# Low parts of one weight matrix on GpSimd, the decoder's first result left in PSUM, a joint first step and a reordered expert stage, in a delta-rule and mixture-of-experts kernel

## The chip, the cores and the metric

One core of a Trainium2 chip runs the whole program. The metric is device time in microseconds (us) of one launch, as a median over runs. Engines: PE is TensorE, PEld its weight load, DVE is VectorE, ACT is ScalarE, POOL is GpSimd, SP is SyncE, which here only issues DMAs.

## What is computed

The reference is a chain of three parts. All inputs arrive as 64-bit floats.

```python
# attention: B, H, S, D = 4, 8, 768, 48, one step per token
k_n = k / (np.linalg.norm(k, axis=-1, keepdims=True) + 1e-06)
for t in range(S):
    y[:, :, t] = np.einsum('bhd,bhde->bhe', q[:, :, t], state)
    v_old = np.einsum('bhde,bhd->bhe', state, kt)
    state = state + bt * np.einsum('bhd,bhe->bhde', kt, vt - v_old)
# first block: x is 3072 x 384, w1 and w2 384 x 1024, w3 1024 x 1024, w_out 1024 x 384
h = (x @ w1) * (x @ w2) @ w3
x = h @ w_out
# second block: 8 experts, the best one for each token
logits = x @ w_gate + modality_bias[modality_id]
e_idx = np.argmax(logits, axis=1)
h = np.maximum(x[mask] @ w1[e], 0.0)
out[mask] = gate_w[mask, None] * (h @ w2[e])
```

## The kernel before, in words

**Engine order.** Every instruction is recorded by a wrapper at line 86, which ties it to the last one of its engine; so each engine keeps the order in which the code was written, and the profile shows L86 for nearly all. A value is kept as two parts, a high one and a low one, and a product takes three matmul passes. ACT casts the high part; the low part is the difference, on DVE (`w34l`, `w`, `sxl`, `hl`, `w2l`, `cl`) or POOL (most of `w1l`).

**Startup** (`startup`, line 553). A list `todo` of 36 tiles of 64-bit words is decoded: tiles 0 to 7 are w_out, the even ones from 8 to 30 and some between are w3, the odd ones from 17 and the last are w1 and w2. `scalar` (line 615) makes on ACT the magnitude `mag` from the high words and the low bits in `out` (shown as `TT`). `vector` (line 631) joins them on DVE with two scalar_tensor_tensor instructions, "the pair" below: the first reads `mag` and `out` and writes `out`, the second reads the raw high words and `out` and writes `out`. `mag` lies in PSUM, for tiles 10 to 32 in a ring "AB" of two buffers. `use` (line 638) folds w3 with w_out into `pw` on PE, or splits a tile of w1 or w2 into its parts; the splits wait in a list `after` that `flush` empties some ticks later. `tick(n)` (line 685) issues: `scalar(n + 1)`, `vector(n)`, the parts that are due, new loads, `use(n)`. The last tile of w3 is tile 30, at the index called `folded`.

**Attention.** 768 tokens go in 12 steps s of 64, for 16 pairs of heads; two steps are a unit, whose triangular matrix `TT` is found on DVE (`tmp`, `Tt`). X[s % 2] holds the state in its first 48 columns and the queries in the other 64 (`queries`, line 409, two DMAs a step). `chain_k` (line 445) multiplies with the keys: for s > 1 state and queries jointly into four PSUM tiles `pkq` (64x112 a matmul), two from the ring `ps` of two buffers, then two from `pc`, also of two. `R` takes the state part, `mask_parts` (line 479) multiplies the query part by a mask on DVE, half of it in slot 0 of the step, half in slot 1. For step 1 state and queries are apart: `pk` in `chain_k`, then `pq` in `masked` (line 417). `chain_u` (`pu`), `chain_y` (`py`) and `chain_s` (`pS`) take both buffers of `pc` each time. POOL's `clear` zeroes 32 rows of X[1] behind the last fold, which had w_out there.

**First block** (`moe1`). Its 12 steps of 8 slots f run beside the attention steps; `slot` (line 167) puts `chain_k` into slot 0, `chain_u` into slot 2 or 3, `chain_y` into 4. The matmuls are `pAB` (9 a matrix) and `px`. Tiles 34 and 35 are decoded in its step 0.

**Second block** (`moe2`, line 1081). 14 slots i of up to 256 tokens of one expert, 8 parts f each (`back`, line 1248): 9 `ph` matmuls, then 6 `spy`. Beside slot i, `ahead` (line 1120) prepares slot i + 1: `weights` splits w1 and w2 of the expert, `tokens2` transposes gathered tokens `xg` (`spt` on PE, `sxh` on ACT, `sxl` on DVE). In slot 0 `late` (line 1086) also places the last tokens: `hot` on DVE, `pl` on PE, `list` on DVE.

Of the kernel before, what the change touches and what calls it, by code (L numbers as in the profile page):

```python
# [8 lines left out]
F32 = mybir.dt.float32  # L9
# [3 lines left out]
I32 = mybir.dt.int32  # L13
# [8 lines left out]
P = 128  # L22
# [83 lines left out]
class Kernel:  # L106
# [60 lines left out]
    def slot(self, s, f):  # L167

        if s >= NS:
            return  # L170
        u, c = divmod(s, US)
        self.at(s + f / FC)
        more = u + 1 < NUNIT
        if f == 0:
            self.chain_k(s)
            if s == 1:
                self.queries(1)
                self.queries(2)
        elif f == 1:
            if c == 0:  # L180
                list(self.merge1(u))
                next(self.work, None)
                if more:
                    self.work = self.inverse(u + 1)
            if s > 1:
                list(self.masks)
        elif f == 2:
            list(self.chain_u(s) if c else self.merge2(u))
            if s == 1:
                list(self.masked(s))  # L190
            if s + 1 < NS:
                self.values(s + 1)
        elif f == 3:
            if c == 0:
                list(self.chain_u(s))
            if c == 1 and u + 2 < NUNIT:
                self.keys(u + 2)
        elif f == 4:
            list(self.chain_y(s))
        elif f == 5:  # L200
            if s + 2 < NS:
                self.queries(s + 2)
            if c == 1 and u + 2 < NUNIT:
                self.prep(u + 2, range(0, NP, HP))
        elif f == 6:
            if s + 1 < NS:
                list(self.chain_s(s))
        elif f == 7:
            if s + 2 < NS:
                self.tokens(s + 2)  # L210
            if c == 1 and u + 2 < NUNIT:
                self.prep(u + 2, range(NP, NU, HP))
# [204 lines left out]
    def masked(self, s):  # L417

        nc, ps = self.nc, self.ps
        kT, W, n0 = self.st[s // US]["kT"], self.st["W", s], s % US * NP  # L420
        mb = self.mask.unsqueeze(1).to_broadcast([P, HP, C])
        todo = []
        for a in range(0, NP, HP):
            pq = ps.tile([P, HP, C], F32, tag="ps", name="pq")
            for n in range(HP):
                for h in range(2):
                    o, w = (1 - h) * C, h * C
                    nc.tensor.matmul(pq[o:o + C, n], kT[w:w + C, n0 + a + n], W[w:w + C, h, a + n], start=True, stop=True)
            todo.append((a, pq))
        yield  # L430
        for a, pq in todo:
            for h in range(2):
                o = (1 - h) * C
                if s < 1:
                    nc.scalar.copy(W[o:o + C, h, a:a + HP], pq[o:o + C])
                    nc.gpsimd.affine_select(out=W[o:o + C, h, a:a + HP], in_=W[o:o + C, h, a:a + HP], pattern=[[0, HP], [1, C]], compare_op=ALU.is_gt, fill=0.0, base=0, channel_multiplier=-1)
                    continue
                nc.vector.tensor_tensor(out=W[o:o + C, h, a:a + HP], in0=pq[o:o + C], in1=mb[o:o + C], op=ALU.mult)

    halves = range(0, NP, HP)  # L440

# [3 lines left out]
    def chain_k(self, s):  # L445

        nc, a1, pc = self.nc, self.a1, self.pc
        kT, n0, vt = self.st[s // US]["kT"], s % US * NP, self.st["v", s]
        self.scaled(s)
        if s == 0:  # L450
            self.R = vt
            return
        X = self.X[self.xi]
        R = a1.tile([P, NP, D], F32, tag="R", name="R")
        if s > 1:
            todo = []
            for q, a in enumerate(range(0, NP, NQ)):
                pool, tag = ((self.ps, "ps"), (pc, "pc"))[q // 2]
                pk = pool.tile([P, NQ, D + C], F32, tag=tag, name="pkq")
                for m in range(NQ):  # L460
                    for h in range(2):
                        o, w = (1 - h) * C, h * C
                        nc.tensor.matmul(pk[o:o + C, m], kT[w:w + C, n0 + a + m], X[w:w + C, h, a + m], start=True, stop=True)
                todo.append((a, pk))
            for a, pk in todo:
                nc.vector.tensor_tensor(out=R[:, a:a + NQ], in0=vt[:, a:a + NQ], in1=pk[:, :, 0:D], op=ALU.subtract)
            self.R = R
            self.masks = self.mask_parts(s, todo)
            next(self.masks)
            return  # L470
        for a in self.halves:
            pk = pc.tile([P, HP, D], F32, tag="pc", name="pk")
            for n, m, h in self.tiles(a):
                o, w = (1 - h) * C, h * C
                nc.tensor.matmul(pk[o:o + C, m], kT[w:w + C, n0 + n], X[w:w + C, h, n, 0:D], start=True, stop=True)
            nc.vector.tensor_tensor(out=R[:, a:a + HP], in0=vt[:, a:a + HP], in1=pk, op=ALU.subtract)
        self.R = R

    def mask_parts(self, s, todo):

        W = self.st["W", s]
        mb = self.mask.unsqueeze(1).to_broadcast([P, NQ, C])
        for q, (a, pk) in enumerate(todo):
            for h in range(2):
                o = (1 - h) * C
                self.nc.vector.tensor_tensor(out=W[o:o + C, h, a:a + NQ], in0=pk[o:o + C, :, D:], in1=mb[o:o + C], op=ALU.mult)
            if q == 1:
                yield
# [72 lines left out]
    def startup(self):  # L561
# [22 lines left out]
        last = {f"w{m}1{kk}": todo.index(("w", (m, 1, kk))) for kk in range(KC) for m in range(2)}  # L584

        free = [f"w{m}1{kk}" for kk in range(KC) for m in range(2)] + ["x0", "x1", "xr"]
        raw, out, mag, after = {}, {}, {}, []
        issued = [0]

        def issue(upto=100):  # L590
# [39 lines left out]

        def vector(n):
            L, Hw, tag = raw.pop(n)
            o, stt = out[n].bitcast(I32), nc.vector.scalar_tensor_tensor
            stt(out=o, in0=mag[n].bitcast(I32), scalar=3, in1=o, op0=ALU.logical_shift_left, op1=ALU.bitwise_or)
            stt(out=o, in0=Hw, scalar=-2147483648, in1=o, op0=ALU.bitwise_and, op1=ALU.bitwise_or)
            if tag != "x0" or n < FC:
                free.append(tag)

        def use(n):
            kind, x = todo[n]  # L640
            due = n + 1 if kind == "w" else min(n + 2, FC) if kind == "o" else n + (2 if n < FC + AHEAD else 4)
            if kind == "o":
                pt = pm.tile([P, KC, P], F32, tag="AB", name="wot", bufs=2)
                for kk in range(KC):
# [12 lines left out]
            elif kind == "3":  # L657
# [6 lines left out]
                if g < half - 1:  # L664
                    return

                def f():
                    nc.scalar.copy(self.w34[0][:, r], pw)
                    nc.vector.tensor_tensor(out=self.w34[1][:, r], in0=pw, in1=self.w34[0][:, r].bitcast(F32), op=ALU.subtract)
            else:  # L670
                m, g, kk = x
                t = wp.tile([P, 2, DCH], F32R, tag=f"w{m}{g}{kk}", name=f"w{m + 1}")
                hi, lo = self.w12[m][0][g][kk], self.w12[m][1][g][kk] = t[:, 0], t[:, 1]

                def f():
                    nc.scalar.copy(hi, out[n])
                    nc.vector.tensor_tensor(out=lo, in0=out[n], in1=hi.bitcast(F32), op=ALU.subtract)
            after.append((due, f))

        def flush(n):  # L680
            now = [f for due, f in after if due <= n]
            after[:] = [x for x in after if x[0] > n]
            for f in now:
                f()

        def tick(n):
            self.n = n
            if n >= NSTART - 2:
                flush(n)
            scalar(n + 1)  # L690
            vector(n)
            flush(n)
            issue()
            use(n)

# [39 lines left out]
            do.setdefault(FC + 8 + x, []).append(lambda: next(rs, None))  # L735
        do.setdefault(t + 4, []).append(lambda: self.parts_x(0))
        folded = todo.index(("3", K3 - 1))
        do.setdefault(folded, []).append(self.clear)
        do.setdefault(folded + 1, []).append(lambda: split(self.chain_s(0)))
        do.setdefault(NSTART - 1, []).extend([lambda: self.tokens(1), lambda: self.tokens(2)])  # L740
        for n in range(-1, NSTART):
# [339 lines left out]
    def moe2(self, early, cur):  # L1081
# [3 lines left out]

        def late():
            yield
            yield from self.place(NT // MT - 1)
            yield
            yield from self.listed()  # L1090
            yield
            yield from self.late_slots()
# [22 lines left out]
        def ahead(i):  # L1115

            self.upto = i + 2
            toks = iter(self.tokens2(todo[i + 1], states[i + 1])) if i + 1 < len(kinds) else iter(())

            def step(tok, n):  # L1120
                for _ in range(n):
                    next(work, None)
                if tok:
                    next(toks, None)

            return step, toks
# [129 lines left out]
    def back(self, i, mi, ahead):  # L1256
# [11 lines left out]
        for f in range(FC):  # L1268
# [9 lines left out]
            hl = s3.tile([P, SLOT], F32R, tag="hl", name="hl", bufs=SLAG + 2)  # L1278
            nc.scalar.activation(hh, ph, AF.Relu)
            nc.vector.scalar_tensor_tensor(out=hl, in0=ph, scalar=0.0, in1=hh.bitcast(F32), op0=ALU.max, op1=ALU.subtract)  # L1280
            ahead(f in (1, 2, 3), 1 + (f < 3 if i == 0 else f > 4))
            if i < NEARLY:
                next(self.late, None)
            elif i > NEARLY + 1:
# [105 lines left out]
```

## Time and profile before

| | us |
|---|---|
| median of 3 runs (lowest to highest) | 841.74 (840.85 to 842.69) |
| the profiled execution | 841.03 |
| its span in the profile | 839.3 |
| around the span | 1.73 |
| PE busy | 786.3 (94%) |
| DVE busy | 618.8 (74%) |
| ACT busy | 408.9 (49%) |
| POOL busy | 165.6 (20%) |

The profiled execution stands 0.71 below the median. The times in the profile count from the start of the span. Startup lasts to about 121, steps 1 to 11 to about 565, and the second block takes the rest. Busy time includes work that overlaps.

### The profile page before, as it was taken

The numbers are of one execution on the slowest core, as the hardware profiler recorded it, in microseconds if no ns is written. First come the engines' busy times: TensorE is split into PE (matmuls) and PEld (weight loads), VectorE is DVE, ScalarE is ACT, GpSimd is POOL, SyncE is SP. The second block draws the span as 40 slices with busy tenths as digits, with TensorE's granted clock in tenths as the row PEclk, the third lists the DMA queues.
The fourth block names the chain that finished last, engine by engine and source line by source line (L and its number), as shares of the span: only waits on it lengthen the run. The fifth ranks groups of instructions, "written<-read, shape, count | busy, mean of one in ns | idle before, by whom it ended". The sixth has DMA issues, their size and how long they took to land.

```text
span 839.3 us, 23624 instructions
## 1 busy us (share of the span) xinstructions
PE 786.3 (94%) x9583; PEld 730.6 (87%) x9583; DVE 618.8 (74%) x1573; ACT 408.9 (49%) x863; POOL 165.6 (20%) x172
## 2 busy tenths in 40 slices
PE   5797789999999999999999999999899999999994
PEld 5664468999999899989998999999799999999983
DVE  5998889769777976897689864567886778677651
ACT  6467673562546154524543353334455655655541
POOL 3021121100000001000100000013254654645420
PEclk8598899999999999999999999999999999999997
DMA  9952563314121421133021401047457678677610
GB/s 310 280 176 87 151 161 102 75 35 120 54 51 38 116 65 40 40 115 82 23 65 39 102 13 31 27 131 222 151 177 246 215 249 258 227 225 238 220 56 6
DMA packets 71812, 105.34 MB, mean 126 GB/s; under 512 B 33988, under 2 KB 53332, under 8 KB 71696
## 3 DMA queue, kind: packets, MB, share of 16 engines
q1 hardware_dynamic: 64464, 88.35, 34.7%
q0 software_dynamic: 4064, 11.06, 3.9%
q10 hardware_dynamic: 3168, 4.34, 1.5%
q8 instruction: 77, 1.26, 0.6%
q14 instruction: 39, 0.32, 0.1%
HBM read 89.15 MB, written 10.63 MB: 119 GB/s over the span
## 4 chain that ended last, share of the span: by engine, by line
PE 46%; DVE 26%; issue 11%; ACT 7%; POOL 4%; DMA 3%; SPq 1%; POOLq 0%; DVEq 0%; ACTq 0%
PE pAB L86 13%; PE px L86 9%; PE ph L86 7%; PE spy L86 4%; DVE tmp L86 4%; DVE Tt L86 4%; DVE X L86 3%; DVE TT L86 2%; PE pw L86 2%; DVE Ab L86 2%; ACT TT L86 2%; PE pkq L86 2%; PE pg L86 2%; DVE a L86 2%; PE py L86 2%
## 5 line engine op out<-in xcount | busy, mean ns | idle before, releaser
L86 PE MATMUL pAB<-x,w 128*128 128x256 f32 x1728 | 228.8, 286 | 0.0
L86 PEld LDWEIGHTS pAB<-x,w 128*128 128x128 f32 x1728 | 213.9, 191 | 4.4
L86 ACT CAST ch<-a 128x256 fp32r<-128x256 f32 x96 | 39.0, 406 | 116.4 <-DVE a L86 116.4
L86 ACT COPY a<-pAB 128x256 f32<-128x256 f32 x96 | 35.6, 371 | 116.9 <-PE pAB L86 104.3
L86 DVE TENSOR_TENSOR a<-a,pAB 128x256 f32<-128x256 f32 x96 | 40.0, 416 | 65.6 <-ACT a L86 65.3
L86 PE MATMUL ph<-sxh,w1h 128*128 128x256 f32 x288 | 82.5, 286 | 0.5 <-DVE hl L86 0.5
L86 ACT ACTIVATE hh<-ph 128x256 fp32r<-128x256 f32 x96 | 37.0, 385 | 91.7 <-PE ph L86 91.5
L86 PE MATMUL ph<-sxl,w1h 128*128 128x256 f32 x288 | 81.2, 282 | 0.0
L86 PE MATMUL ph<-sxh,w1l 128*128 128x256 f32 x288 | 81.2, 282 | 0.0
L86 DVE SCALAR_TENSOR_TENSOR hl<-ph,hh 128x256 fp32r<-128x256 f32 x96 | 40.3, 420 | 41.0 <-ACT hh L86 40.5
L86 DVE TENSOR_TENSOR Tt<-tmp,Tt 128x31 f32<-128x31 f32 (+15 forms) x186 | 64.3, 346 | 6.4
L86 DVE TENSOR_TENSOR w2l<-r,w2h 128x768 fp32r<-128x768 f32 x56 | 59.5, 1074 | 12.2 <-ACT w2h L86 11.9
L86 DVE TENSOR_TENSOR tmp<-Ab,Tt 128x31 f32<-128x31 f32 (+15 forms) x186 | 65.4, 352 | 3.0
L86 PE MATMUL px<-w34h,ch 128*128 128x392 f32 x192 | 65.6, 342 | 0.0
L86 PE MATMUL px<-w34h,cl 128*128 128x392 f32 x192 | 65.3, 340 | 0.0
L86 PE MATMUL px<-w34l,ch 128*128 128x392 f32 x192 | 65.2, 339 | 0.0
L86 POOL TENSOR_TENSOR w1l<-r,w1h 128x512 fp32r<-128x512 f32 x39 | 51.0, 1327 | 49.9 <-ACT w1h L86 49.6
L86 DVE TENSOR_TENSOR cl<-a,ch 128x256 fp32r<-128x256 f32 x96 | 43.0, 447 | 20.1 <-ACT ch L86 19.3
L86 PEld LDWEIGHTS ph<-sxh,w1h 128*128 128x128 f32 x288 | 54.7, 190 | 1.3 <-DVE hl L86 1.1
L86 PEld LDWEIGHTS ph<-sxh,w1l 128*128 128x128 f32 x288 | 54.8, 190 | 0.0
L86 PEld LDWEIGHTS ph<-sxl,w1h 128*128 128x128 f32 x288 | 54.6, 190 | 0.0
L86 ACT CAST w1h<-r 128x512 fp32r<-128x512 f32 x84 | 49.5, 615 | 2.9 <-DMA r<-in_e_w_dram 2.5
(269 smaller groups left out, 1677.7 us busy)
## 6 DMA issues: line engine op xcount, KB each, us to landing
r<-in_e_w_dram SPq DMA_DIRECT2D x42, 512.0 KB, 4.7
r<-in_e_w_dram SPq DMA_DIRECT2D x56, 384.0 KB, 3.9
raw<-in_w_dram SPq DMA_DIRECT2D x28, 512.0 KB, 4.6
kT<-in_kt_dram SPq DMA_DIRECT2D x12, 512.0 KB, 4.5
X<-in_q_dram SPq DMA_DIRECT2D x24, 256.0 KB, 4.8
vt<-in_v_dram SPq DMA_DIRECT2D x12, 384.0 KB, 4.7
kb<-in_kb_dram SPq DMA_DIRECT2D x12, 384.0 KB, 4.7
x2d<-xr ACTq DMA_DIRECT2D x22, 192.5 KB, 2.8
```

The lines of the kernel that those rows point to most:

```text
L86: x = f(*a, **kw)
```

## The change

1. In `vector` the first result of the decoder stays in `mag`, in place, and the second instruction reads it there. Tiles from 33 on keep `mag` in SBUF.
2. In `tick` the high parts that are due stand ahead of that tick's `mag` and `TT` on ACT; the low parts still follow the pair.
3. The low parts of w1's tiles 17, 21, 25 and 29 go to POOL.
4. The queries of steps 1 and 2 are fetched right behind tile 30. Step 1 is joint too (`pkq`), and its mask is a copy on ACT and an affine_select on POOL in place of DVE's product.
5. The four `pkq` tiles come from `ps`, `ps`, `pc`, `pc` in even steps and from `pc`, `pc`, `ps`, `ps` in odd steps.
6. In the second block `pl` and `list` of slot 0 come one f later; in slot 0 the tokens of slot 1 stand ahead of its weights; in slot 2 the transposes are at f = 3, 4, 5 in place of 1, 2, 3.

```diff
 def slot(self, s, f):
         if f == 0:
             self.chain_k(s)
-            if s == 1:
-                self.queries(1)
-                self.queries(2)
...
-            if s > 1:
-                list(self.masks)
+            list(self.masks)
...
-            if s == 1:
-                list(self.masked(s))
...
 def chain_k(self, s):
-            pool, tag = ((self.ps, "ps"), (pc, "pc"))[q // 2]
+            pool, tag = ((self.ps, "ps"), (pc, "pc"))[(q // 2 + s) % 2]
...
 def mask_parts(self, s, todo):
+                if s == 1:
+                    self.nc.scalar.copy(W[o:o + C, h, a:a + NQ], pk[o:o + C, :, D:])
+                    self.nc.gpsimd.affine_select(out=W[o:o + C, h, a:a + NQ], in_=W[o:o + C, h, a:a + NQ], pattern=[[0, NQ], [1, C]], compare_op=ALU.is_gt, fill=0.0, base=0, channel_multiplier=-1)
+                    continue
...
 def vector(n):
-            stt(out=o, in0=mag[n].bitcast(I32), scalar=3, in1=o, op0=ALU.logical_shift_left, op1=ALU.bitwise_or)
-            stt(out=o, in0=Hw, scalar=-2147483648, in1=o, op0=ALU.bitwise_and, op1=ALU.bitwise_or)
+            stt(out=m, in0=m, scalar=3, in1=o, op0=ALU.logical_shift_left, op1=ALU.bitwise_or)
+            stt(out=o, in0=Hw, scalar=-2147483648, in1=m, op0=ALU.bitwise_and, op1=ALU.bitwise_or)
...
+                low.append((n + 1, lambda: (nc.gpsimd if not m and n < NSTART - 3 else nc.vector).tensor_tensor(out=lo, in0=out[n], in1=hi.bitcast(F32), op=ALU.subtract)))
...
 def tick(n):
+            for f in due(n, (high,)):
+                f()
             scalar(n + 1)
             vector(n)
-            flush(n)
+            for f in due(n, (low, after)):
+                f()
             issue()
             use(n)
...
-        do.setdefault(folded, []).append(self.clear)
+        do.setdefault(folded, []).extend([self.clear, lambda: self.queries(1), lambda: self.queries(2)])
...
 def late():
             yield
-            yield from self.place(NT // MT - 1)
+            last = self.place(NT // MT - 1)
+            next(last)
             yield
+            next(last)
+            yield
+            yield
+            list(last)
             yield from self.listed()
...
 def step(tok, n):
+                if tok and i == 0:
+                    next(toks, None)
                 for _ in range(n):
                     next(work, None)
-                if tok:
+                if tok and i > 0:
                     next(toks, None)
...
-            ahead(f in (1, 2, 3), 1 + (f < 3 if i == 0 else f > 4))
+            ahead(f - 2 * (i == 2) in (1, 2, 3), 1 + (f < 3 if i == 0 else f > 4))
```

SP at the end of startup, where it issues the last loads of raw words (`raw`), the keys of later steps (`kb`) and the queries (X_91 is X[1], for step 1, and X_90 is X[0], for step 2):

```order
 L86 DMA vt<-in_v_dram 128x768
-L86 DMA raw<-in_w_dram 128x512 x13
-L86 DMA kb<-in_kb_dram 128x768 x2
+L86 DMA raw<-in_w_dram 128x512 x12
 L86 DMA X_91<-in_q_dram 64x16x64 x2
 L86 DMA X_90<-in_q_dram 64x16x64 x2
+L86 DMA raw<-in_w_dram 128x512
+L86 DMA kb<-in_kb_dram 128x768 x2
```

The four loads of queries have moved ahead of the last raw tile and of two loads of keys, which now stand behind them.

POOL in startup, behind the stores of step 0's output (`x<-yT`); the names w_... are w1's tiles, TT_94 holds decoded tiles:

```order
 L86 DMA x<-yT 32x256
+L86 TENSOR_TENSOR w_1034<-TT_94,w_1034 128x512
+L86 TENSOR_TENSOR w_1087<-TT_94,w_1087 128x512
+L86 TENSOR_TENSOR w_1124<-TT_94,w_1124 128x512
 L86 MEMSET X_91 32x32x48 x2
 L86 TENSOR_TENSOR vt<-vt,rb 128x768
+L86 AFFINE_SELECT X_91<-X_91 64x4x64 x8
```

Three of the four low parts now stand between the stores and the zeroing of X[1], and the eight selects of step 1 behind it.

DVE in slot 0 of the second block, from the comparisons `hot` of the last tokens to the `list` that is made of them:

```order
 L86 TENSOR_SCALAR hot<-cols,hi 128x192
 L86 SCALAR_TENSOR_TENSOR hl<-ph,hh 128x256
-L86 TENSOR_TENSOR w2l<-r,w2h 128x768
-L86 TENSOR_TENSOR sxl<-spt,sxh 128x256
+L86 TENSOR_TENSOR sxl<-spt,sxh 128x256
+L86 TENSOR_TENSOR w2l<-r,w2h 128x768
+L86 SCALAR_TENSOR_TENSOR hl<-ph,hh 128x256
+L86 TENSOR_TENSOR w2l<-r,w2h 128x768
 L86 TENSOR_TENSOR list<-pl,list 128x192
-L86 SCALAR_TENSOR_TENSOR hl<-ph,hh 128x256
-L86 TENSOR_TENSOR w2l<-r,w2h 128x768
 L86 TENSOR_SCALAR shift<-list 128x192
```

Here `sxl` has moved ahead of `w2l`, and `list` behind one more `hl` and `w2l`.

## Rows read from the trace of the kernel before

**Rows 1.** The page: span, busy time of each engine

```profile
span 839.3 us, 23624 instructions
...
PE 786.3 (94%) x9583; PEld 730.6 (87%) x9583; DVE 618.8 (74%) x1573; ACT 408.9 (49%) x863; POOL 165.6 (20%) x172
```

**Rows 2.** Windows: stretch and length; busy PE, PEld, DVE, ACT, POOL; granted clock; DMA

```profile
57.00:121.00 64.00, 49.82 (x666) 31.60 (x666) 55.09 (x108) 44.24 (x81) 12.73 (x25) 0.89 0.45 141
159.00:565.00 406.00, 400.68 (x6214) 381.23 (x6214) 303.22 (x914) 175.18 (x373) 17.89 (x16) 1.00 0.22 60
...
597.00:601.00 4.00, 3.86 (x18) 3.92 (x18) 1.89 (x5) 0.00 (x0) 0.00 (x0) 0.57 0.54 215
```

**Rows 3.** Waits of PE from 120 to 560: us in total, times, longest

```profile
PE pu L86 <- DVE X L86: 4.1, 4, 1.4
PE py L86 <- DVE X L86: 1.6, 3, 1.0
PE pkq L86 <- DVE list L86: 1.0, 2, 0.6
```

**Rows 4.** Timeline of PE, step 3: start, length; idle before in brackets

```profile
200.02 3.37 PE L86 MATMUL pkq<-X,kT 64*64 64x112 f32 x64
...
210.93 2.07 PE L86 MATMUL pu<-R,TT 64*64 64x48 f32 x64 [0.88 <-DVE X L86]
```

**Rows 5.** Timeline of DVE, step 3: the masks of slots 0 and 1

```profile
205.94 1.73 DVE L86 TENSOR_TENSOR X<-pkq,mask 64x256 f32<-64x256 f32 x4
...
209.93 1.74 DVE L86 TENSOR_TENSOR X<-pkq,mask 64x256 f32<-64x256 f32 x4
```

**Rows 6.** Timeline of PE in slots 0 and 2 of the second block

```profile
592.13 0.44 PE L86 MATMUL spt<-ident,xg 128*128 128x128 f32 x2 [1.15 <-DVE sxl L86]
...
596.75 0.64 PE L86 MATMUL pl<-hot 128*128 128x192 f16 x2 [1.84 <-DVE hot L86]
...
632.04 0.33 PE L86 MATMUL spt<-ident,xg 128*128 128x128 f32 x1 [1.59 <-DMA xg<-x2d,id]
```

**Rows 7.** Timeline of DVE and of POOL in slot 0 of the second block

```profile
594.19 1.23 DVE L86 TENSOR_SCALAR hi<-hi 128x2 f32<-128x2 f32 x1
595.54 0.42 DVE L86 SCALAR_TENSOR_TENSOR hl<-ph,hh 128x256 fp32r<-128x256 f32 x1
...
591.07 4.30 POOL L86 TENSOR_TENSOR w1l<-r,w1h 128x512 fp32r<-128x512 f32 x3
```

**Rows 8.** Waits of DVE, then of ACT, from 57 to 121

```profile
DVE w34l L86 <- ACT w34h L86: 3.7, 3, 2.7
DVE w L86 <- ACT w L86: 2.4, 2, 1.8
...
ACT mag L86 <- DVE TT L86: 7.3, 7, 1.7
```

**Rows 9.** Groups of DVE by form (57 to 121; whole): busy, mean ns, idle before

```profile
L86 DVE SCALAR_TENSOR_TENSOR TT<-mag,TT 128x512 int32<-128x512 int32 x19 | 12.9, 682 | 0.0
...
L86 DVE TENSOR_TENSOR w<-TT,w 128x512 fp32r<-128x512 f32 x12 | 8.2, 686 | 4.1 <-ACT w L86 4.1
L86 DVE TENSOR_TENSOR w34l<-pw,w34h 128x392 fp32r<-128x392 f32 x8 | 4.5, 562 | 4.2 <-ACT w34h L86 4.2
```

**Rows 10.** Timeline of DVE: a decoder instruction at 118 and step 1's masks

```profile
118.29 1.59 DVE L86 SCALAR_TENSOR_TENSOR TT<-raw,TT 128x512 int32<-128x512 int32 x1
...
136.06 2.85 DVE L86 TENSOR_TENSOR X<-pq,mask 64x512 f32<-64x512 f32 x4
```

**Rows 11.** Timeline of PE: the fold of tile 30, and step 1

```profile
113.93 0.93 PE L86 MATMUL pw<-X,TT 128*128 128x392 f32 x2 [0.36 <-DVE TT L86]
...
118.81 2.12 PE L86 MATMUL pk<-X,kT 64*64 64x48 f32 x64 [0.41 <-ACT X L86]
```

**Rows 12.** The tile X from 145 to 420: its loads

```profile
DMA to landing us min/median/max: 3.8/4.6/5.7
```

**Rows 13.** Groups of POOL by form: step 0's selects

```profile
L86 POOL TENSOR_SCALAR_AFFINE_SELECT X<-X 64x512 f32<-64x512 f32 x4 | 3.1, 785 | 45.4 <-ACT X L86 45.2
```

More of the change, by code (lines that the diff above doesn't have):

```diff
@@ L420, in masked @@
         kT, W, n0 = self.st[s // US]["kT"], self.st["W", s], s % US * NP
-        mb = self.mask.unsqueeze(1).to_broadcast([P, HP, C])
         todo = []
@@ L433, in masked @@
                 o = (1 - h) * C
[L434 to L438, printed above, removed]
+                nc.scalar.copy(W[o:o + C, h, a:a + HP], pq[o:o + C])
+                nc.gpsimd.affine_select(out=W[o:o + C, h, a:a + HP], in_=W[o:o + C, h, a:a + HP], pattern=[[0, HP], [1, C]], compare_op=ALU.is_gt, fill=0.0, base=0, channel_multiplier=-1)
     halves = range(0, NP, HP)
@@ L454, in chain_k @@
         R = a1.tile([P, NP, D], F32, tag="R", name="R")
-        if s > 1:
-            todo = []
-            for q, a in enumerate(range(0, NP, NQ)):
-                pool, tag = ((self.ps, "ps"), (pc, "pc"))[q // 2]
[L459 to L476, printed above, removed]
+        todo = []
+        for q, a in enumerate(range(0, NP, NQ)):
+            pool, tag = ((self.ps, "ps"), (pc, "pc"))[(q // 2 + s) % 2]
+            pk = pool.tile([P, NQ, D + C], F32, tag=tag, name="pkq")
+            for m in range(NQ):
+                for h in range(2):
+                    o, w = (1 - h) * C, h * C
+                    nc.tensor.matmul(pk[o:o + C, m], kT[w:w + C, n0 + a + m], X[w:w + C, h, a + m], start=True, stop=True)
+            todo.append((a, pk))
+        for a, pk in todo:
+            nc.vector.tensor_tensor(out=R[:, a:a + NQ], in0=vt[:, a:a + NQ], in1=pk[:, :, 0:D], op=ALU.subtract)
         self.R = R
+        self.masks = self.mask_parts(s, todo)
+        next(self.masks)
     def mask_parts(self, s, todo):
@@ L586, in startup @@
         free = [f"w{m}1{kk}" for kk in range(KC) for m in range(2)] + ["x0", "x1", "xr"]
-        raw, out, mag, after = {}, {}, {}, []
+        raw, out, mag, after, high, low = {}, {}, {}, [], [], []
         issued = [0]
@@ L632, in vector @@
             L, Hw, tag = raw.pop(n)
-            o, stt = out[n].bitcast(I32), nc.vector.scalar_tensor_tensor
-            stt(out=o, in0=mag[n].bitcast(I32), scalar=3, in1=o, op0=ALU.logical_shift_left, op1=ALU.bitwise_or)
-            stt(out=o, in0=Hw, scalar=-2147483648, in1=o, op0=ALU.bitwise_and, op1=ALU.bitwise_or)
+            o, m, stt = out[n].bitcast(I32), mag[n].bitcast(I32), nc.vector.scalar_tensor_tensor
+            stt(out=m, in0=m, scalar=3, in1=o, op0=ALU.logical_shift_left, op1=ALU.bitwise_or)
+            stt(out=o, in0=Hw, scalar=-2147483648, in1=m, op0=ALU.bitwise_and, op1=ALU.bitwise_or)
             if tag != "x0" or n < FC:
@@ L640, in use @@
             kind, x = todo[n]
-            due = n + 1 if kind == "w" else min(n + 2, FC) if kind == "o" else n + (2 if n < FC + AHEAD else 4)
+            when = min(n + 2, FC) if kind == "o" else n + (2 if n < FC + AHEAD else 4)
             if kind == "o":
@@ L665, in use @@
                     return
-                def f():
-                    nc.scalar.copy(self.w34[0][:, r], pw)
-                    nc.vector.tensor_tensor(out=self.w34[1][:, r], in0=pw, in1=self.w34[0][:, r].bitcast(F32), op=ALU.subtract)
+                high.append((when, lambda: nc.scalar.copy(self.w34[0][:, r], pw)))
+                low.append((when, lambda: nc.vector.tensor_tensor(out=self.w34[1][:, r], in0=pw, in1=self.w34[0][:, r].bitcast(F32), op=ALU.subtract)))
+                return
             else:
@@ L673, in use, with due @@
                 hi, lo = self.w12[m][0][g][kk], self.w12[m][1][g][kk] = t[:, 0], t[:, 1]
[L675 to L678, printed above, removed]
+                high.append((n + 1, lambda: nc.scalar.copy(hi, out[n])))
+                low.append((n + 1, lambda: (nc.gpsimd if not m and n < NSTART - 3 else nc.vector).tensor_tensor(out=lo, in0=out[n], in1=hi.bitcast(F32), op=ALU.subtract)))
+                return
+            after.append((when, f))
+        def due(n, lists):
+            for x in lists:
+                now = [y for y in x if y[0] <= n]
+                x[:] = [y for y in x if y[0] > n]
+                yield from (f for _, f in now)
         def flush(n):
-            now = [f for due, f in after if due <= n]
-            after[:] = [x for x in after if x[0] > n]
-            for f in now:
+            for f in due(n, (after, high)):
+                f()
+            for f in due(n, (low,)):
                 f()
@@ L689, in tick @@
                 flush(n)
+            for f in due(n, (high,)):
+                f()
             scalar(n + 1)
             vector(n)
-            flush(n)
+            for f in due(n, (low, after)):
+                f()
             issue()
```

## The prediction, made blind

> **What bounds the kernel.** I read the page first, for the busy shares, then windows over the stages, then the waits of PE, and last the timelines around each wait. PE is busy 786.3 of 839.3 us [rows 1], and the windows show where it is not [rows 2]: in the long middle, 159 to 565, it stands only 5.3 of 406 us, while in startup, 57 to 121, it is busy 49.8 of 64 and DVE 55.1. So one microsecond less on PE's path in the middle or in the second block is one microsecond less of the whole, but in startup PE follows DVE's decoder, and only what makes DVE's row of work shorter counts there, up to the fold of tile 30 and the first product of step 1. [...]
>
> The sum goes against the profiled execution, 841.03 us; the median of the runs is 0.71 above it, and I add that at the end.
>
> **Term 1, the rings by step: -5.1.** In the middle, PE waited four times for a mask product of DVE before `pu`, 4.1 in all, and twice before `pkq` for `list`, 1.0 [rows 3]. The place in step 3: `pu` began at 210.93 after 0.88 idle [rows 4], because both buffers of `pc` held the second half of `pkq`, whose masks DVE made only in slot 1, from 209.93 to 211.67; the masks of the first half were made from 205.94 [rows 5]. With `pc` first in odd steps, `pu` needs the masks of slot 0, which end at 207.67, 3.3 before `pu` starts. So the wait is gone in all four odd steps (the longest is 1.4, still under 3.3). What is late next: `R` is made ahead of those masks, and the next product on DVE that PE needs stands behind the second masks as before, with a product of PE between. The second waits, 1.0, are for a `ps` buffer at the beginning of `pkq`; in odd steps `ps` is now asked for half of `pkq` later, 3.37 / 2 = 1.7 [rows 4], more than their longest, 0.6. Both go: -4.1 - 1.0. Upper end: only the four go and a new wait of the second kind takes 1.0 back in the others, -3.1.
>
> **Term 2, slot 0 of the second block: -3.2.** PE stood 1.15 before `spt` at 592.13 and 1.84 before `pl` at 596.75 [rows 6]. The second is for `hot`, which DVE had behind tiny operations that took 1.23 in place of a few tenths while POOL made three `w1l` from 591.07 to 595.37 [rows 7]. One f later `hot` is long made: -1.84. For `spt`, `sxl` no longer stands behind a `w1l`, a difference of 512 columns like `w`, 0.69 [rows 9]; I take -0.6 of 1.15. The clock of 0.57 over 4.0 us [rows 2] costs 4.0 x 0.43 = 1.7, and I count it back, because the long standing ahead of it goes. Against it: those tiny operations stay on DVE, and `hl` behind them was ready only at 595.54 + 0.42 [rows 7], so that PE meets it where `pl` covered it before; I take +0.9. -1.84 - 0.6 - 1.7 + 0.9 = -3.2; ends -5.3 (both waits and the clock cost, nothing new) and -1.5.
>
> **Term 3, slot 2: -1.6.** The transpose at 632.04 waited 1.59 for the gathered rows [rows 6]. Two f later it is asked for well after: from the transposes at 592.13 to the end of those of the next f, at 596.75 - 1.84, one f took 2.8 [rows 6]. Ends -1.6 and 0 (if `sxl` of the last transposes is late for slot 3).
>
> **Term 4, startup and step 1: -2.5.** Its parts, on DVE's row of work first.
> - High parts first: DVE waited 3.7 in three for `w34h` and 2.4 in two for `w` [rows 8], each time behind a cast that ACT had put after `mag` and `TT`. The cast itself stays; I take it as long as its difference on DVE, 0.56 or 0.69 [rows 9]: 6.1 - 3 x 0.56 - 2 x 0.69 = 3.0 goes. Ends -6.1 and 0.
> - Low parts on POOL: three of the four (tiles 17, 21, 25) stand ahead of the fold of tile 30 on DVE, 3 x 0.69 [rows 9] = -2.1. POOL takes 4.30 / 3 = 1.43 for such a one [rows 7], and none of them is needed before the first block. But a POOL operation can hold DVE up: a decoder instruction that runs 0.68 [rows 9] took 1.59 at 118.29 [rows 10], while POOL worked on `vt`. The first of the four falls beside DVE's `tmp` and `Tt`, which read two SBUF operands; the others mostly beside decoder pairs, which now read one. I take one full block, +1.4.
> - The decoder's result in PSUM. No row shows DVE writing PSUM in place. The nearest are reads of PSUM: `w34l`, 392 columns from PSUM, takes 562, and `w`, 512 columns from SBUF, 686 [rows 9]; 124 ns for 120 columns, about 1 ns a column, leaves nothing for PSUM. So 0 a tile. [...] But `mag`'s buffer comes free one instruction later; I take +0.7 for it (once), the rest being rival two.
> - Step 1. Before, `pk` began 118.81 - 113.93 = 4.9 after the last fold's first piece [rows 11]. Now the queries are loaded into X[1] as soon as that piece has read it, 0.93 later, by two issues; a load lands 3.8 to 5.7 after its issue [rows 12]. 0.93 + 5.7 and a little for the second issue makes 7.0, so `pkq` is 2.1 later. Being joint it takes 3.37 [rows 4] in place of twice some 2.12 [rows 11]: -0.9. Together +1.2, between -0.9 (loaded in time) and +3.2 (landing at 9).
> - Step 1's masks: 2.85 leave DVE [rows 10], and with them PE's three waits of 1.6 before `py` [rows 3]. ACT's copies have room. POOL's selects were 785 ns for 512 columns [rows 13], so eight of half that are 3.1; they read SBUF and may hold DVE: I take one block, 1.59 - 0.68 = +0.9. Ends 0 and +3.1.
> - SP: the four issues pass one raw tile and two `kb`. The raw tile is decoded in the first block's step 0, the keys are used later still; with a landing under 6 [rows 12] nobody waits.
>
> -3.0 - 2.1 + 1.4 + 0.7 + 1.2 - 1.6 + 0.9 = -2.5. Ends: -7.6 (nothing held, queries in time: -3.0 - 2.1 - 0.9 - 1.6) and +3.5.
>
> [...]
>
> **Sum.** 841.03 - 5.1 - 3.2 - 1.6 - 2.5 = 828.6, and 0.7 for the median: **829.3 us**.
>
> **Rival one: POOL holds DVE every time.** Each of the four low parts costs DVE POOL's 1.43 in place of its own 0.69, and the selects their 3.1. Term 4: -3.0 + 4 x 1.43 - 3 x 0.69 + 0.7 + 1.2 - 1.6 + 3.1 = +4.0, less what falls beside decoder pairs; I take +3.2, and the time is 835. For it: 118.29 [rows 10] and the tiny operations under `w1l` [rows 7]. [...]
> [...]
>
> **Rival two, slower: the ring of `mag` turns ACT and DVE into a row.** `mag(n + 2)` has to wait for the second instruction of tile n in place of the first. If DVE then waits for ACT at each of the 23 tiles in the ring, 0.69 a tile, startup gets 23 x 0.69 = 15.9 longer. The point from which it decides: ACT's cast, `mag` and `TT` behind a pair must take longer than DVE's next pair and low part, and a low part taken off DVE moves it that way. 841.74 - 9.9 (terms 1 to 3) + 15.9 - 3.0 + 1.2 = 846. Against it: DVE never waited for `mag` in 19 tiles (idle before 0.0 [rows 9]), and ACT waited for DVE seven times, 7.3 [rows 8], so ACT had room of 1.0 a time.
>
> **Rival three: all of term 4 comes**, with queries in time and nothing held: 829.3 - 5 = 824 to 826.
>
> **Rival four: the rings only move the wait.** The buffers of `ps` come late for what else uses them in odd steps, and term 1 gives nothing: 834. Against it: both gains rest on differences of several tenths to 2 us.
>
> **Numbers.** A measurement of this kernel can tell 0.2%, 1.7 us, from no change. The forecast, 827 to 832, has 0.55; rival one (832 to 837) 0.20; rival three 0.12; rival four 0.05; rival two 0.06; no change 0.02. The range 824.5 to 836.5 takes in the forecast and rivals one, three and four. Faster 0.92, same 0.02, slower 0.06.
>
> **What the profile after would show.** Term 1: no wait of `pu` for X from 160 to 560, and `pkq` not waiting for `list`. Term 2: no idle before `pl`, clock near 1.00 around 600. Term 3: no wait of `spt` for a DMA. Term 4: DVE idle for `w34h` and `w` under 3 us, the last fold a few us earlier, `pkq` of step 1 starting about 7 after it, no wait before `py` of step 1. I am wrong if DVE waits for `mag` in startup, if `tmp` and `Tt` take three times their length under POOL's low parts, or if PE stands in the middle as before under another name.

## The result, and the profile after

The changed kernel takes 832.10 us (median of 4 runs, 831.20 to 832.57) against 842.22 for the kernel before in the same count: ratio 0.988, interval 0.9863 to 0.9898, 10.1 us less. The forecast was 829.3 with a range of 824.5 to 836.5: faster, as foretold, by a fifth less. The profiled execution took 832.43, 8.6 below that of before (841.03); the sum had promised 12.4. The page, which answers to [rows 1]:

```profile
span 830.7 us, 23501 instructions
...
PE 784.3 (94%) x9519; PEld 728.0 (88%) x9519; DVE 616.5 (74%) x1567; ACT 410.8 (49%) x871; POOL 176.4 (21%) x184
```

To see where the 8.6 lie, the same instructions of PE in both kernels serve as marks: the last fold of tile 30, the product behind `py` of step 1, the first `ph` of slots 0, 1 and 2, and the first product of 512 columns in the half slot. The timeline of PE before:

```profile
140.04 2.42 PE L86 MATMUL pAB<-x,w 128*128 128x256 f32 x18
...
586.62 0.28 PE L86 MATMUL ph<-sxh,w1h 128*128 128x256 f32 x1
...
610.33 0.28 PE L86 MATMUL ph<-sxh,w1h 128*128 128x256 f32 x1
...
628.04 0.28 PE L86 MATMUL ph<-sxh,w1h 128*128 128x256 f32 x1
...
805.94 0.86 PE L86 MATMUL ph<-w1h,sxh 128*128 128x512 f32 x3
```

and after:

```profile
113.57 0.93 PE L86 MATMUL pw<-X,TT 128*128 128x392 f32 x2 [0.42 <-DVE TT L86]
...
139.27 2.41 PE L86 MATMUL pAB<-x,w 128*128 128x256 f32 x18
...
579.99 0.28 PE L86 MATMUL ph<-sxh,w1h 128*128 128x256 f32 x1
...
600.59 0.28 PE L86 MATMUL ph<-sxh,w1h 128*128 128x256 f32 x1
...
618.30 0.28 PE L86 MATMUL ph<-sxh,w1h 128*128 128x256 f32 x1
...
797.33 0.86 PE L86 MATMUL ph<-w1h,sxh 128*128 128x512 f32 x3
```

The differences of neighbouring marks, with 113.93 of [rows 11] as the first of before:

| stretch | before | after | difference | foretold |
|---|---|---|---|---|
| to the fold of tile 30 | 113.93 | 113.57 | -0.4 | -3.0 |
| to the product behind `py` | 26.11 | 25.70 | -0.4 | +0.5 |
| to slot 0 | 446.58 | 440.72 | -5.9 | -5.1 |
| slot 0 | 23.71 | 20.60 | -3.1 | -3.2 |
| slot 1 | 17.71 | 17.71 | 0.0 | 0 |
| slot 2 to the half slot | 177.90 | 179.03 | +1.1 | -1.6 |

The first stretch also holds the scatter of the first tiles (the second decoder instruction of the 4th tile ends between 17.90 and 19.93 in 13 profiles), so its -0.4 can't be told from nothing. So two terms came, and in this execution two did not. PE's waits from 120 to 560 (us in total, times, longest) show the first that came; `pu` and `list` of [rows 3] are gone:

```profile
PE pkq L86 <- DMA X<-in_q_dram: 0.9, 1, 0.9
PE pkq L86 <- ACT An L86: 0.8, 2, 0.4
```

and the windows the second: the middle has 0.4 us of idle PE in place of 5.3, and around 600 the granted clock is 1.00 where it was 0.57 [rows 2].

```profile
159.00:565.00 406.00, 405.64 (x6258) 386.91 (x6259) 306.98 (x930) 178.33 (x381) 23.40 (x20) 1.00 0.23 64
...
597.00:601.00 4.00, 4.00 (x28) 4.00 (x27) 3.76 (x15) 0.89 (x2) 0.00 (x0) 1.00 0.62 212
```

**Startup.** POOL's timeline has the low parts of tiles 17 and 21, DVE's what ran beside them:

```profile
76.53 1.54 POOL L86 TENSOR_TENSOR w<-TT,w 128x512 fp32r<-128x512 f32 x1 [12.54 <-ACT w L86]
...
95.09 1.29 POOL L86 TENSOR_TENSOR w<-TT,w 128x512 fp32r<-128x512 f32 x1
```

```profile
76.86 1.26 DVE L86 COPY Tt<-bt 128x32 f32<-128x32 f32 x1
...
94.32 0.41 DVE L86 TENSOR_TENSOR tmp<-Ab,Tt 128x240 f32<-128x240 f32 x1
94.77 1.88 DVE L86 TENSOR_TENSOR Tt<-tmp,Tt 128x240 f32<-128x240 f32 x1
```

A copy of 32 columns, 0.19 without a neighbour (the third experiment), took 1.26, and `Tt` 1.88 where its twin `tmp` took 0.41: 2.5 us lost to two low parts that save 1.4. The other two low parts, at 106.30 and 112.86, held nothing: they fell beside decoder pairs and a `w34l`, which kept their 0.69 and 0.56. And of DVE's waits [rows 8], those for `w34h` fell from 3.7 to 1.5, but those for `w` rose from 2.4 to 6.2:

```profile
DVE w L86 <- ACT w L86: 6.2, 2, 4.7
DVE w34l L86 <- ACT w34h L86: 1.5, 1, 1.5
```

The 4.7 is new: the cast of tile 31 now stands behind ACT's copies of step 0's state (at 117.43), which wait for POOL's zeroing. The other, 1.55 before `w` of tile 19, is an old one of 1.75. ACT's timeline says why it stayed: the cast stood not behind `mag` and `TT`, but behind a copy that itself waited for PE (at 86.70).

```profile
86.70 1.94 ACT L86 COPY X<-pu 64x384 f32<-64x384 f32 x4 [5.48 <-PE pu L86]
88.54 0.62 ACT L86 CAST w<-TT 128x512 fp32r<-128x512 f32 x1
...
117.43 1.95 ACT L86 COPY X<-pS 48x384 f32<-48x384 f32 x4 [2.40 <-POOL X L86]
119.41 0.62 ACT L86 CAST w<-TT 128x512 fp32r<-128x512 f32 x1
```

**Step 1.** PE reaches `pkq` 6 us after the fold, waits, and waits again for the second half of the queries:

```profile
119.56 0.37 PE L86 MATMUL pkq<-X,kT 64*64 64x112 f32 x2 [1.52 <-DMA X<-in_q_dram]
120.84 3.25 PE L86 MATMUL pkq<-X,kT 64*64 64x112 f32 x62 [0.91 <-DMA X<-in_q_dram]
```

120.84 - 113.57 = 7.3, where 7.0 was foretold; from there to the end of step 1 PE waits for nothing, `py` included. POOL's selects held DVE for little: beside the second four, `tmp` and `Tt` took at most 0.51 in place of 0.42, and it was the selects that got longer.

```profile
125.64 1.84 POOL L86 TENSOR_SCALAR_AFFINE_SELECT X<-X 64x256 f32<-64x256 f32 x4 [6.67 <-ACT X L86]
131.34 2.43 POOL L86 TENSOR_SCALAR_AFFINE_SELECT X<-X 64x256 f32<-64x256 f32 x4 [3.86 <-ACT X L86]
```

**Slot 0.** `pl` waits for nothing, and `spt` waits 0.54 for `sxl` in place of 1.15. What is left is a wait for `hl`, behind tiny operations of DVE that run beside POOL's `w1l`; DVE, then PE:

```profile
586.74 0.98 DVE L86 TENSOR_TENSOR pos<-pos,oh 128x16 f32<-128x16 f32 x1
...
587.96 1.04 DVE L86 TENSOR_SCALAR hi<-pf 128x2 f32<-128x2 f32 x1
...
589.79 0.39 PE L86 MATMUL ph<-sxh,w1h 128*128 128x256 f32 x1 [1.08 <-DVE hl L86]
```

**Slot 2.** The transposes no longer wait for gathered rows. But DVE, POOL, ACT and PE, each in its timeline, show what is late instead:

```profile
627.46 3.77 DVE L86 TENSOR_TENSOR w2l<-r,w2h 128x768 fp32r<-128x768 f32 x1 [0.30 <-ACT w2h L86]
631.15 0.41 DVE L86 TENSOR_TENSOR sxl<-spt,sxh 128x256 fp32r<-128x256 f32 x1
```

```profile
627.85 2.54 POOL L86 TENSOR_TENSOR w1l<-r,w1h 128x512 fp32r<-128x512 f32 x2
```

```profile
634.82 0.62 ACT L86 CAST w1h<-r 128x512 fp32r<-128x512 f32 x1 [2.74 <-DMA r<-in_e_w_dram]
```

```profile
635.78 0.44 PE L86 MATMUL spy<-w2h,hh 128*128 128x384 f32 x1 [0.40 <-ACT hh L86]
...
641.06 0.39 PE L86 MATMUL ph<-sxh,w1h 128*128 128x256 f32 x1 [1.22 <-DVE hl L86]
```

A `w2l` took 0.95 at 591.45, where POOL did nothing. In the kernel before, the first one of this slot took 1.77:

```profile
639.28 1.77 DVE L86 TENSOR_TENSOR w2l<-r,w2h 128x768 fp32r<-128x768 f32 x1 [0.30 <-ACT w2h L86]
```

Here, beside two `w1l` of POOL, it took 3.77; it and they hold buffers of raw weights, so the next load comes late (issued at 631.25, `w2l` having ended at 631.23), ACT waits 2.74 for it with `hh` queued behind, and PE waits at the end of slot 2 and in slot 3.

### The profile page after: what moved, and what is told of

Its sections match the earlier page's. It is cut to its first block, busy times and chain, and to the rows that moved or that the text cites. A ratio compares the mean times of both kernels' runs of the same rounds, so it can differ in the third digit from the quotient of the medians.

```text
span 830.7 us, 23501 instructions
## 1 busy us (share of the span) xinstructions
PE 784.3 (94%) x9519; PEld 728.0 (88%) x9519; DVE 616.5 (74%) x1567; ACT 410.8 (49%) x871; POOL 176.4 (21%) x184
## 3 DMA queue, kind: packets, MB, share of 16 engines
q8 instruction: 77, 1.26, 0.6%
## 4 chain that ended last, share of the span: by engine, by line
PE 69%; issue 8%; POOL 4%; DMA 2%; DVE 2%; ACT 1%; POOLq 0%; SPq 0%; DVEq 0%
PE pAB L86 26%; PE px L86 16%; PE ph L86 7%; PE pkq L86 4%; PE spy L86 3%; PE py L86 3%; PE pu L86 3%; PE pS L86 2%; PE pg L86 2%; POOL w1l L86 2%; POOL out_dram L86 1%; PE pf L86 1%; PE pe L86 1%; POOL xg L86 1%; DMA r<-in_e_w_dram 1%
## 5 line engine op out<-in xcount | busy, mean ns | idle before, releaser
L86 DVE TENSOR_TENSOR cl<-a,ch 128x256 fp32r<-128x256 f32 x96 | 40.6, 423 | 20.1 <-ACT ch L86 19.3
```

Source lines behind the costliest of these rows:

```text
L86: x = f(*a, **kw)
```

## The experiments

"Tiles" is from the end of the second decoder instruction of the 4th tile to that of the 31st, since the first tiles scatter by up to 2.0 us from run to run; "slot 0" and "slot 2 on" are the stretches of the table above. These three are of one profiled execution each; us is the median of all timed runs, and the ratio is to the kernel before timed beside them (842.22 for the changed kernel, 840.26 to 840.55 for runs 1 to 12). A us of one row and that of another differ by this too, so both columns have to be read.

| run | us | ratio (interval) | tiles | slot 0 | slot 2 on |
|---|---|---|---|---|---|
| before | 842.22 | | 95.5 | 23.7 | 177.9 |
| changed | 832.10 | 0.988 (0.9863 to 0.9898) | 95.4 | 20.6 | 179.0 |
| 1 rings alone | 834.51 | 0.9925 (0.9909 to 0.9942) | 96.5 | 23.7 | 178.2 |
| 2 slot 2 back | 832.41 | 0.9908 (0.9893 to 0.9924) | 94.6 | 20.6 | 177.9 |
| 3 lows on DVE | 830.60 | 0.9884 (0.9866 to 0.9903) | 93.9 | 20.6 | 178.0 |
| 4 step 1 back | 834.89 | 0.9932 (0.9916 to 0.9949) | 95.5 | 20.6 | 176.2 |
| 5 pair back | 830.99 | 0.9889 (0.987 to 0.9909) | 95.6 | 20.6 | 176.3 |
| 6 high parts late | 834.25 | 0.9929 (0.9907 to 0.9952) | 97.2 | 20.6 | 176.2 |
| 7 shift by one | 830.70 | 0.9889 (0.9869 to 0.991) | 94.7 | 20.6 | 177.2 |
| 8 slot 3's w1l on DVE | 830.61 | 0.9884 (0.9862 to 0.9906) | 95.6 | 20.6 | 176.2 |
| 9 POOL's differences on DVE | 827.99 | 0.9848 (0.9824 to 0.9873) | 92.9 | 19.5 | 176.3 |
| 10 `pl` and `list` back | 836.89 | one run | 96.2 | 24.1 | 177.2 |
| 11 as 9, high parts first | 827.06 | 0.9829 (0.981 to 0.9848) | 92.8 | 19.5 | 176.2 |
| 12 changed, again | 831.49 | 0.9879 (0.9859 to 0.99) | 95.5 | 20.6 | 177.7 |

**1. The kernel before with the rings alone.**

```diff
-            pool, tag = ((self.ps, "ps"), (pc, "pc"))[q // 2]
+            pool, tag = ((self.ps, "ps"), (pc, "pc"))[(q // 2 + s) % 2]
```

> The kernel before with the rings by step alone. Theory (term 1 of the prediction: the waits of pu and pkq in odd steps go and nothing follows): 5 to 6 us less than before, about 836.5, no wait of pu for X between 160 and 560, the first transposes of the second block 5 to 6 us earlier. Rival (the wait moves to another consumer of the two rings): 840 or more, with a new wait of PE of 3 us or more in 160 to 560.

Its waits of PE from 120 to 560:

```profile
PE py L86 <- DVE X L86: 1.7, 3, 1.1
PE pk L86 <- ACT X L86: 0.4, 1, 0.4
PE pkq L86 <- ACT An L86: 0.2, 1, 0.2
```

The stretch from the product behind `py` to slot 0 was 440.6, 6.0 less than before, and the median is 5.9 below that of the kernel before: the theory, and the rival falls.

**2. Slot 2's transposes back.**

```diff
-            ahead(f - 2 * (i == 2) in (1, 2, 3), 1 + (f < 3 if i == 0 else f > 4))
+            ahead(f in (1, 2, 3), 1 + (f < 3 if i == 0 else f > 4))
```

> The changed kernel with slot 2's transposes back at f = 1, 2, 3. Theory from its trace (the later transposes put a w2l beside two w1l of POOL, it takes 3.8 in place of 0.95, loads of weights start late and slot 3 waits): 1 us less than the changed kernel, about 831, a wait of spt for the gathered rows of 1.6, and no wait of spy for hh or of ph for hl of over 1 us around 636 to 641. Rival (term 3 of the prediction as it stands): 1.6 more, about 833.7.

In the profile as the theory had it, 1.1 less from slot 2 on, and the wait is back on PE:

```profile
622.36 0.33 PE L86 MATMUL spt<-ident,xg 128*128 128x128 f32 x1 [1.61 <-DMA xg<-x2d,id]
```

But the median is not 1 below the changed kernel's; by the ratios the run is some 2 us slower, with intervals that just overlap, which is nearer the rival. What the profiled execution of the changed kernel lost does not happen in all: seven profiles with the shift and POOL's `w1l` (the changed kernel twice, and 3, 4, 5, 6, 10) took 176.2 to 179.0, 177.2 in the mean, and the three without the shift 177.9 to 178.2.

**3. Low parts on DVE.**

```diff
-low.append((n + 1, lambda: (nc.gpsimd if not m and n < NSTART - 3 else nc.vector).tensor_tensor(
+low.append((n + 1, lambda: nc.vector.tensor_tensor(
...
```

> The changed kernel with all low parts of w1 back on DVE. Theory from its trace (two of POOL's four held a DVE operation, 1.1 and 1.5, which is what three low parts save): within 0.7 of the changed kernel, the fold of tile 30 within 0.7 of 113.6. Rival one (the prediction's: they save 2.1 and cost 1.4): 0.7 more. Rival two (POOL costs DVE more than is seen): 1 to 2 less.

The copy that took 1.26 is back at its own length:

```profile
76.61 0.19 DVE L86 COPY Tt<-bt 128x32 f32<-128x32 f32 x1
```

The tiles took 93.9, and 92.9 and 92.8 in runs 9 and 11, which have this edit too, against 94.6 to 96.2 in seven profiles with the startup as changed (the changed kernel twice, and 2, 4, 7, 8, 10): by the tiles it is rival two, with 2.2 between the means. In that stretch DVE was busy for 85.1 in the mean of the three, with three more differences, against 85.9 in the seven, and idle for 8.1 against 9.5: most of the 2.2 is idle time that went, and no run shows what ended it. The whole doesn't decide: the median of run 3 is 0.9 to 1.5 below the changed kernel's, the ratio is the same (0.9884 against 0.988).

**4. Step 1 as before.** The edit undoes point 4 of the change; one part of it:

```diff
-        do.setdefault(folded, []).extend([self.clear, lambda: self.queries(1), lambda: self.queries(2)])
+        do.setdefault(folded, []).append(self.clear)
...
```

> The changed kernel with step 1 as in the kernel before (queries fetched in slot 0 of step 1, pk and pq apart, the mask on DVE). Theory from the traces (the joint step is 1.7 behind at pu and 0.4 ahead at the product after py, counted from the last fold): 0.4 more, about 832.5; pAB of slot 0 about 3.5 earlier, py waiting for X 1.6. Rival (the late load of the queries is what the joint step costs): 1 us or more less.

From the fold to the product behind `py` it took 28.6, where the changed kernel took 25.7 and the kernel before 26.1: both expectations of the time fall. The masks' products lie behind DVE's new wait for tile 31, and `py` waits longer than in the kernel before. DVE, then PE:

```profile
121.47 0.69 DVE L86 TENSOR_TENSOR w<-TT,w 128x512 fp32r<-128x512 f32 x1 [4.68 <-ACT w L86]
...
139.59 0.30 PE L86 MATMUL py<-X 128*64 128x64 f32 x2 [2.41 <-DVE X L86]
```

So, as these timelines have it, the joint step of the changed kernel hides a delay of DVE that the other parts made; no run takes that delay away with step 1 as before.

**5. The decoder's pair as before.**

```diff
-            stt(out=m, in0=m, scalar=3, in1=o, op0=ALU.logical_shift_left, op1=ALU.bitwise_or)
-            stt(out=o, in0=Hw, scalar=-2147483648, in1=m, op0=ALU.bitwise_and, op1=ALU.bitwise_or)
+            stt(out=o, in0=m, scalar=3, in1=o, op0=ALU.logical_shift_left, op1=ALU.bitwise_or)
+            stt(out=o, in0=Hw, scalar=-2147483648, in1=o, op0=ALU.bitwise_and, op1=ALU.bitwise_or)
```

> The changed kernel with the decoder's pair as before (first result to SBUF, mag's buffer free after the first instruction). Counted from the fourth decoded tile to the 31st, since the first tiles' loads scatter: the changed kernel took 94.6 to 95.5 in three runs, the kernel before 95.5 and 96.5. Theory from the traces (in PSUM every second pair starts its second instruction 0.78 after its first in place of 0.72, and ACT waits longer for mag): 0.5 to 1 less. [...] Rival two (the prediction's slower one: the ring makes a row of ACT and DVE): 5 or more less.

95.6, inside the range of those seven profiles: what leaving the result in PSUM is worth can't be told from nothing. The theory of a gain by undoing it isn't borne out, and the prediction's slower rival falls.

**6. High parts late.**

```diff
-            for f in due(n, (high,)):
-                f()
             scalar(n + 1)
             vector(n)
+            for f in due(n, (high,)):
+                f()
```

> The changed kernel with the high parts behind mag and TT again on ACT. Counted as for the pair, from the fourth tile to the 31st. Theory (the order of the casts is worth 0.7, the only stretch that got shorter, 13th to 21st tile): 0.5 to 1 more. Rival (the prediction's 3.0): 3 more. DVE's waits for w34h and w from 57 to 121 go up by as much.

97.2, some 1.8 above the mean of the seven, which lie 1.6 apart: more than the theory, less than the rival. The whole is 2.2 above the changed kernel's 832.10 by the median and some 4 by the ratio, so it doesn't rule the rival out.

**7. A shift by one.**

```diff
-            ahead(f - 2 * (i == 2) in (1, 2, 3), 1 + (f < 3 if i == 0 else f > 4))
+            ahead(f - (i == 2) in (1, 2, 3), 1 + (f < 3 if i == 0 else f > 4))
```

> The changed kernel with slot 2's transposes at f = 2, 3, 4. From the start of slot 2 to the products of 512 columns of the first half slot the kernel before took 177.9, the changed one 179.0, a run in which nothing collided 176.2. Theory (the gathered rows are there after one f, and whether w2l meets POOL's w1l depends on single us): between 176.2 and 178, no wait of spt for the rows over 0.3. Rival (one f is not enough): spt still waits, 177 or more for that reason.

177.2; `spt` waited 0.4 for the rows, and a `w2l` took 3.27. One f all but suffices for the rows, and does not avoid the collision.

**8. The w1l of slot 3's expert on DVE.**

```diff
-                (nc.vector if i == 0 or kk * W1N + n < W1D else nc.gpsimd)
+                (nc.vector if i in (0, 3) or kk * W1N + n < W1D else nc.gpsimd)
```

> The changed kernel with the three w1l that POOL makes for slot 3's expert on DVE. Theory (POOL's w1l is what holds w2l in slot 2, and the loads behind it): w2l 0.96 each, 176.2 from the start of slot 2 to the half slot, 2.8 less than the changed kernel. Rival (three more operations of 0.69 make DVE as late as before, or something else holds w2l): w2l over 1.5, 178 or more.

DVE in slot 2, with the same order otherwise:

```profile
628.28 0.96 DVE L86 TENSOR_TENSOR w2l<-r,w2h 128x768 fp32r<-128x768 f32 x1 [0.30 <-ACT w2h L86]
```

176.2, PE waits for nothing from 600 to 680, and runs 9 and 11, which have this edit too, took 176.3 and 176.2. That POOL's `w1l` is the cause of slot 2's loss is shown. Without the edit 176.2 comes too, when the meeting is a milder one: in runs 4, 5 and 6 the first `w2l` was over in 0.96, and the next two took 2.71 to 2.87 in place of 1.83. Run 5:

```profile
629.94 2.73 DVE L86 TENSOR_TENSOR w2l<-r,w2h 128x768 fp32r<-128x768 f32 x2 [0.30 <-ACT w2h L86]
```

By the ratio the whole of run 8 is not told from the changed kernel (0.9884 against 0.988).

**9 and 11. A version of its own.** Run 9 joins run 3, run 8 and the `w1l` of slot 1's expert on DVE (`i in (0, 1, 3)`); run 11 also takes the high parts ahead of other late work:

```diff
-            for f in due(n, (after, high)):
+            for f in due(n, (high, after)):
```

> The changed kernel with all low parts of w1 on DVE in startup, and with the w1l of the experts of slots 1 and 3 on DVE. Theory (POOL's differences held DVE at each of these places): fourth tile to 31st about 93.9 in place of 95.2, slot 0 no longer than 20.6 and up to 1 shorter (pos, hi and w1l at their usual 0.2 and 0.7), slot 2 to the half slot 176.2; the whole 829 or a little less, 2 to 4 below the changed kernel. Rival (DVE has no room for six more operations of 0.69): slot 0 longer than 20.6, the whole no better than the changed kernel.

> The version before (low parts and six w1l on DVE), and in the last ticks the high parts ahead of the copies of the state on ACT. Theory (PE has no wait in step 1 but for the queries' load, so DVE's 4.7 for w there is hidden): within 0.5 of that version. Rival (DVE's delay there reaches PE by a later product): 1 to 2 less, and pkq of step 2 without its wait for An of 0.8.

In slot 0 of run 9 the tiny operations, 0.98 (`pos`) and 1.04 (`hi`) in the changed kernel and 1.01 and 1.23 (two `hi`) in the one before, are back at:

```profile
585.04 0.17 DVE L86 TENSOR_TENSOR pos<-pos,oh 128x16 f32<-128x16 f32 x1
...
585.45 0.17 DVE L86 TENSOR_SCALAR hi<-pf 128x2 f32<-128x2 f32 x1
```

Slot 0 takes 19.5, and both versions beat both kernels: 827.06 and 827.99, 13.5 and 12.6 below the 840.55 of the kernel before on the same chip, where the changed kernel stood at 831.49. The interval of run 11 lies clear of the changed kernel's, that of run 9 overlaps it a little. Between the two nothing is decided: run 11's median is 0.9 lower, `pkq` of step 2 still waits 0.7 for `An`, and in its profile step 1 takes 1.2 longer: 62 products of `pkq` take 4.91 where they take 3.25 in run 9. PE had stood about as long ahead of them in both (1.33 and 0.77; 1.25 and 0.85), so why they took longer stays open.

**10. `pl` and `list` back where they were.**

```diff
-            last = self.place(NT // MT - 1)
-            next(last)
-            yield
-            next(last)
-            yield
-            yield
-            list(last)
+            yield from self.place(NT // MT - 1)
+            yield
```

> The changed kernel with pl and list of slot 0 where they were, the tokens still ahead of the weights. Theory (the wait for hot and the clock that falls after it are what term 2 gained): slot 0 takes 23 to 24 in place of 20.6, pl waits 1.5 or more, granted clock under 0.8 behind it. Rival (the order of tokens and weights is what helped): slot 0 under 22.

Slot 0 takes 24.1, the wait is 2.8, and the window behind it has a clock of 0.73:

```profile
593.04 0.72 PE L86 MATMUL pl<-hot 128*128 128x192 f16 x2 [2.82 <-DVE hot L86]
```

```profile
594.00:599.00 5.00, 5.00 (x28) 5.00 (x27) 2.13 (x5) 1.11 (x2) 0.00 (x0) 0.73 0.42 140
```

With the order of tokens and weights alone the gain is gone: `spt` waits 0.55 in place of 1.15, but `pl` waits 2.82 in place of 1.84. So term 2 needs the new place of `pl`; whether the place alone would give all of it was not run.

**12. The changed kernel again.**

> The changed kernel once more, beside the two before. Theory (whether w2l of slot 2 meets POOL's w1l depends on single us): 830 to 832.5, and from slot 2 to the half slot 176.2 to 179.1, with w2l from 0.96 to 3.8. Rival (the collision is fixed by the order): 179.0 again.

177.7 with a `w2l` of 3.73: neither the 179.0 of the first profile nor the 176.2 of runs 4 to 6. What the collision costs varies.

## Why the prediction was right, and where it was not

- **Term 1, -5.1: right, a little small.** The stretch gave 5.9, and the rings alone 6.0. The waits of `pu` and of `pkq` for `list` went and nothing of their size took their place, so rival four is out. In the trace of after `pkq` of step 2 waits 0.8 for ACT's `An`, which was 0.2 before.
- **Term 2, -3.2: right, 3.1, and by its parts.** The wait of `pl` went, that of `spt` fell by 0.6, the clock stayed at 1.00, and the new wait that it set against the gain, for `hl`, came at 1.08 (0.9 foretold).
- **Term 3, -1.6: the step that failed was what is late next.** The sum named `sxl` for slot 3; it was the `w2l` behind the moved transposes. The old order met POOL's `w1l` for less (a `w2l` of 1.77 there): +1.1 in the profile in place of -1.6. Runs 4, 5 and 6 show about the -1.6, where the meeting is milder (176.2 against 177.9), and the mean of the seven profiles with the shift is 0.8 below the three without it: in the mean the term had the right sign and half the size.
- **Term 4, -2.5: the failed step is the low parts on POOL.** "I take one full block, +1.4" against -2.1 saved; it was two, 1.07 and 1.47, and the tiles of runs 3, 9 and 11 show that the move costs about 2 in place of gaining 0.7. The two blocks explain some 0.5 of it, 2.5 against 2.1; the rest is mostly idle time of DVE, whose cause stays open. The block fell on `tmp` and `Tt`, where the second low part was expected beside decoder pairs: it stood behind the stores on POOL's queue until 95. The prediction had named this as a sign of being wrong, `tmp` and `Tt` at three times their length; `Tt` took more than four times. High parts first seems over-sized: 1.8 by the tiles of run 6, one profile, where 3.0 was taken from waits of which one belonged to `X<-pu`. The block of 0.9 for the selects did not come. The queries' load was right (7.3 for 7.0), and so was the loss of `py`'s waits. Together -0.8. In the sum itself, the upper end of +3.5 is less than the 4.7 to which the upper ends of the parts add up.
- **Rival one was the half of the truth that the sum left out.** POOL held DVE in startup (`Tt` 1.88 where `tmp` took 0.41), in slot 0 (`hi` 1.04 where run 9 has 0.17) and in slot 2 (`w2l` 3.77 where run 8 has 0.96), but not at every place, so the time is 832 and not 835. The rival's +3.2 in place of +4.0, for what falls beside decoder pairs, was the author's estimate; so was the one full block of term 4, next to which the text counts the SBUF operands of DVE's instructions, and no run shows that their number decides. With one input, the copy of 32 columns took 1.26 and `hi` 1.04 beside POOL. The decoder's second instruction kept its 0.69 beside POOL with one SBUF operand (112.83 in the changed kernel), and with two in run 5 (106.56).
- **The chances** put 0.55 on 827 to 832; 832.10 lies just beyond it, at the near end of rival one's 832 to 837, and the second count of the changed kernel, 831.49, just inside. Terms 3 and 4, and POOL in both, put it there.

## What to carry to other kernels

Before an elementwise operation goes to GpSimd, list what VectorE does in the same microseconds: here ten differences taken back from GpSimd brought some 3.5 us (run 9 against run 12), though VectorE then did more work. Where work is moved to let a transfer land, look at what it pushes, and at which buffers that holds (here a `w2l` of 3.77, and a wait of 2.74 for the load behind it). Where two consumers share two rings, ask which half is freed first, and give the next user that ring (6.0 us in run 1).

## What was not expected of the hardware

A DVE instruction that had begun first was held all the same: `w2l` began at 627.46, POOL's pair at 627.85, and `w2l` ended at 631.23, 0.84 after POOL did at 630.39; `Tt` began at 94.77, POOL at 95.09, and ended 0.27 after it. By the starts that the profile shows, coming first by 0.3 or 0.4 did not help there. In run 5, with both operands of the decoder's second instruction in SBUF again, it went the other way: that instruction came first by 0.10 and kept its 0.69, and POOL's difference took 1.75, where those at 106.30 and 112.86 in the changed kernel took 1.28 and 1.29. So the starts shown do not tell which engine will be held. DVE, then POOL, in run 5:

```profile
106.56 0.69 DVE L86 SCALAR_TENSOR_TENSOR TT<-raw,TT 128x512 int32<-128x512 int32 x1
...
106.66 1.75 POOL L86 TENSOR_TENSOR w<-TT,w 128x512 fp32r<-128x512 f32 x1 [9.85 <-DMA raw<-in_w_dram]
```

A decoder instruction that writes PSUM in place took 0.69 (112.05 in the changed kernel), as long as the one that writes SBUF behind it. On tiles of 512 columns up to 116 the second started 0.72 to 0.80 after the first in the changed kernel, and 0.69 to 0.72 after it in the kernel before, where both write SBUF; no more was seen of a price of PSUM.
